# Retention, then SwiGLU on one core: operand stores a block earlier, a ring of four, wide float64 conversion

## The chip, the cores and the metric

One core of a Trainium2 chip runs the whole program. The metric is the device time of an execution in microseconds (us). Engines are named as in the profile: PE multiplies matrices, DVE, ACT and POOL work on elements, SP issues most of the DMAs.

## The reference

Two stages follow each other. For each of 4 batches and 8 heads the first carries a 64x64 state over 768 steps; the second is a SwiGLU block on 3072 rows of 512.

```python
for t in range(S):                       # q, k, v: (4, 8, 768, 64), float32
    state = gamma * state + outer(k[t], v[t])
    y[t] = scale * q[t] @ state          # gamma differs by head
x = y.transpose(0, 2, 1, 3).reshape(3072, 512)
g = x @ w_gate                           # 512 x 1536
out = (g / (1 + exp(-g)) * (x @ w_val)) @ w_out   # 1536 x 512
```

The three weights arrive as float64, everything else as float32.

## The kernel before

Retention runs on chunks of 128 steps. A segment is three chunks of two batches (six chunks, 768 rows of `xT`), and there are four segments. Each segment has a retention stage, an up stage of 12 blocks (one per 128 of the 1536 columns, `up`) and a down stage of three row groups (`down`). The retention of segment s+1 is cut into steps and put between the products of the down stage of segment s; that of segment 0 runs alone at the start.

The products are written as a Strassen-like scheme of seven: `up` multiplies seven operands (slots of a `wt` tile of 7 x 256) with seven activation operands (parts of `xT` and their sums `xs`, made in `sums_x`). In this text the products of a block are called by their order: first to seventh. First, third, fifth and seventh add into the PSUM tile `x`, second and fourth into `w`, sixth is `z`. Because `x` is added to again, the third product waits until ACT has copied the first result (`p1`), and the seventh until DVE has read `x` at line 381.

The float64 weights must become float32, and the slots that are sums must be formed. This happens in segment 0 only: a finished `wt` is stored to DRAM (`wstore`) and loaded again in segments 1 to 3 (`kept_wt`). A piece of 128x512 doubles is loaded as pairs of 32-bit words (`raw`), and `convert_piece` makes floats of it: one ACT operation on the low words (line 151), four on DVE (lines 153, 154, 158, 159) and an integer addition on POOL (line 161). `sums_t` then makes four sums on POOL (line 170). An up block has two such pieces (`w_gate`, `w_val`), and a half of a down operand `wot` (`w_out`) goes with it. `fill` puts these steps into the blocks of segment 0; each engine and each DMA queue works its instructions in the order of the program. `wt` tiles come from a ring of three, `raw` from a ring of two, and the store of block f's operands is issued after block f's products (line 487).

Of the kernel before, what the change touches and what calls it, by code (L numbers as in the profile page):

```python
# [37 lines left out]
def tile_retnet_swiglu(  # L38
# [45 lines left out]
    first = early.__enter__()  # L84
    ctx.enter_context(tc.manual_schedule())
# [36 lines left out]
    landed = {}  # L122

    def load_piece(n, dst, src):

        if src.dtype == F32:
            if len(src.shape) == 3:
                dst = dst.rearrange("p (c f) -> p c f", c=NC)
            nc.sync.dma_start(out=dst, in_=src)
            return  # L130
        raw = raws.tile([P, 2 * NC * P], U32, tag="raw", name=f"raw_{n}")
        to = raw.rearrange("p (c f) -> p c f", c=NC) if len(src.shape) == 3 else raw
        nc.sync.dma_start(out=to, in_=src.bitcast(U32))
        landed[n] = raw

    def convert_piece(n, dst):

        if n not in landed:
            return []
        raw = landed.pop(n).rearrange("p (n two) -> p n two", two=2)
        lo, hi = raw[:, :, 0], raw[:, :, 1]
        d = dst.bitcast(U32)

        def first_():  # L150
            nc.scalar.activation(lo.bitcast(F32), lo, AF.Copy, scale=2.0 ** -51,
                                 bias=2.0)
            nc.vector.tensor_scalar(d, hi, 0x7FFFFFFF, None, op0=ALU.bitwise_and)  # L153
            nc.vector.tensor_scalar(dst, dst, 122879.9921875, 2.0 ** -15,  # L154
                                    op0=ALU.min, op1=ALU.max)

        def second():
            nc.vector.tensor_scalar(hi, hi, 0x80000000, None, op0=ALU.bitwise_and)  # L158
            nc.vector.scalar_tensor_tensor(d, d, 3, hi, op0=ALU.logical_shift_left,  # L159
                                           op1=ALU.bitwise_xor)  # L160
            nc.gpsimd.tensor_tensor(dst.bitcast(I32), dst.bitcast(I32),  # L161
                                    lo.bitcast(I32), op=ALU.add)
        return [first_, second]

    def sums_t(w, b12):

        b11, b21, b22 = w[:, 0], w[:, 3 - b12], w[:, 3]
        t1, t3, t2, t4 = w[:, b12], w[:, 4], w[:, 5], w[:, 6]
        for o, a, b in ((t3, b22, t1), (t1, t1, b11), (t2, b22, t1), (t4, b21, t2)):
            nc.gpsimd.tensor_tensor(o, a, b, op=ALU.subtract)  # L170

    pieces = []

    def up_source(w, f):
        return w[:, ts(f, P)].rearrange("(c p) f -> p c f", p=P)

    for f in range(NF):
        pieces.append((f, 0, up_source(w_gate, f)))
        pieces.append((f, 1, up_source(w_val, f)))
    down_pieces = []  # L180
    for j in range(FH):
        for i in range(2):
            down_pieces.append((j, i, w_out[ts(j + FH * i, P)]))

    order = []
    for f in range(NF):
        order += [("up",) + pieces[2 * f], ("up",) + pieces[2 * f + 1]]
        order.append(("down",) + down_pieces[f])

    def place(n):  # L190
        kind, a, i, _ = order[n]
        if kind == "up":
            w = wt[0, a] if (0, a) in wt else new_wt(0, a)
        else:
            w = wot[a]
        return w, w[:, ds(2 * i, 2)].rearrange("p a b -> p (a b)")

    AHEAD = 2
    n_loaded = [0]

    def load_next():
        n = n_loaded[0]
        if n < len(order):
            n_loaded[0] += 1
            load_piece(n, place(n)[1], order[n][3])

    def steps_of_piece(n):

        kind, a, i, _ = order[n]

        def after():
            for s in todo[n]:
                s()
            load_next()
            if i == 1:
                sums_t(place(n)[0], 2 if kind == "up" else 1)

        todo = {}

        def one():  # L220
            steps = convert_piece(n, place(n)[1])
            todo[n] = steps[1:]
            for s in steps[:1]:
                s()
        return [one, after]

    fillers = [step for n in range(len(order)) for step in steps_of_piece(n)]

    def fill(k):
        for _ in range(min(k, len(fillers))):  # L230
            fillers.pop(0)()
# [48 lines left out]
    def state(c):  # L280
        ci = c % NCK
        if ci == NCK - 1:
            return
        kd = att.pop((c, "kd"))
        vn = chunks[c][3]
        st = bank("st", 1, f"st_{c}")
        for n in range(NP):
            nc.tensor.matmul(st[:, ts(n, P)], kd[:, ds(2 * n, 2)], vn[:, ts(n, P)],  # L288
                             start=(n == 0), stop=True, skip_group_check=True)
        new, old = state_of(c), state_of(c, 1)  # L290
        for i in range(2):
# [27 lines left out]
    def retention(s):  # L319
# [12 lines left out]
        for n, c in enumerate(cs):  # L332
# [3 lines left out]
            steps.append(lambda n=n: last(n))  # L336
        return steps
# [5 lines left out]
    def sums_x():  # L343
        s1, s2, s3, s4 = xs
        tt = nc.vector.tensor_tensor
        tt(s1, a_up(1, 0), a_up(1, 1), op=ALU.add)  # L346
        tt(s2, s1, a_up(0, 0), op=ALU.subtract)
        tt(s4, a_up(0, 1), s2, op=ALU.subtract)
        tt(s3, a_up(0, 0), a_up(1, 0), op=ALU.subtract)

    def up(s, f, fill):
# [10 lines left out]
        def tmp(nm):  # L362
            return io.tile([P, TH], F32, tag=nm, name=f"{nm}_{s}_{f}")
# [15 lines left out]
        tt(hT[:, f, 0], wb, u2, op=add)  # L379
        product(x, 4, s3, start=False)  # L380
        tt(hT[:, f, 1], x, p5, op=add)  # L381
        z = bank("wz", 2, f"z_{s}_{f}")[:, :TH]
        product(z, 1, a_up(0, 1))
        c11 = tmp("c11")
        tt(c11, z, p1, op=add)  # L385
        nc.scalar.activation(c11, c11, AF.Silu)  # L386
        fill(1)
        product(x, 6, a_up(1, 1), start=False)
        tt(hT[:, f, 0], hT[:, f, 0], c11, op=mul)  # L389
        sg = tmp("sg")  # L390
        nc.scalar.activation(sg, x, AF.Silu)
        fill(1)
        tt(hT[:, f, 1], hT[:, f, 1], sg, op=mul)
# [17 lines left out]
    def down(s, u, step):  # L411
# [10 lines left out]
        def tmp(nm):  # L422
            return io.tile([P, TH], F32, tag=nm, name=f"d{nm}_{s}_{u}")[:, :DH]
# [9 lines left out]
        product(x, 0, a_dn(0, 0, u))  # L433
        p1 = tmp("p1")
        nc.scalar.copy(p1, x)
        product(wb, 1, cur[1])
        p5 = tmp("p5")
        nc.scalar.copy(p5, wb)
        product(x, 5, cur[2], start=False)
        u2 = tmp("u2")  # L440
        nc.scalar.copy(u2, x)
        product(wb, 3, cur[4], start=False)
        tt(ev[0][:, DH:], wb, u2, op=ALU.add)
        more(1, 2, 4)
        product(x, 4, cur[3], start=False)
# [3 lines left out]
        product(z, 2, a_dn(0, 1, u))  # L449
        tt(ev[0][:, :DH], z, p1, op=ALU.add)  # L450
        product(x, 6, a_dn(1, 1, u), start=False)
# [10 lines left out]
    for n in range(1, len(cs)):  # L462
        load_chunk(cs[n], first, str(n))
        if n == 2:
            for _ in range(AHEAD):
                load_next()
    steps = retention(0)
    for n, st in enumerate(steps):
        st()
        if n >= 8 and n % 2 == 0 and len(fillers) > 2 * (len(order) - 6):  # L470
            fill(1)
    fill(len(fillers) - 2 * (len(order) - 6))
    sums_x()
# [3 lines left out]

    for s in range(NSEG):
        nxt = seg_chunks(s + 1) if s + 1 < NSEG else []
        for f in range(NF):  # L480
            if s:
                if f + 2 < NF:
                    kept_wt(s, f + 2)
            w = wt[s, f]
            up(s, f, fill if s == 0 else lambda k: None)
            if s == 0:
                nc.sync.dma_start(out=wstore[f], in_=w)
# [5 lines left out]

        def step():
            if steps:
                steps.pop(0)()

        for u in range(L):
# [3 lines left out]
            down(s, u, step)  # L502
        while steps:
            steps.pop(0)()
        if nxt:
            sums_x()
# [49 lines left out]
```

## Time and profile before

| what | us |
|---|---|
| median of 3 runs (877.7 to 881.0) | 880.84 |
| profiled execution, its own time | 879.36 |
| its span, first to last instruction | 877.6 |
| PE busy in the span | 780.5 |
| DVE, ACT, POOL busy | 372.9, 173.3, 158.1 |

The span is 1.76 us short of the execution's own time. Times in the rows are from the start of the span. The line numbers are those of the kernel before, except where the changed kernel is spoken of. A PEclk of 1.00 is 2.4 GHz and 0.50 is 1.2 GHz.

### The profile page before, as it was taken

The numbers are of one execution on the slowest core, as the hardware profiler recorded it, in microseconds if no ns is written. First come the engines' busy times: TensorE is split into PE (matmuls) and PEld (weight loads), VectorE is DVE, ScalarE is ACT, GpSimd is POOL, SyncE is SP. The second block draws the span as 40 slices with busy tenths as digits, with TensorE's granted clock in tenths as the row PEclk, the third lists the DMA queues.
The fourth block names the chain that finished last, engine by engine and source line by source line (L and its number), as shares of the span: only waits on it lengthen the run. The fifth ranks groups of instructions, "written<-read, shape, count | busy, mean of one in ns | idle before, by whom it ended". The sixth has DMA issues, their size and how long they took to land.

```text
span 877.6 us, 8898 instructions
## 1 busy us (share of the span) xinstructions
PE 780.5 (89%) x3440; PEld 542.7 (62%) x3440; DVE 372.9 (42%) x604; ACT 173.3 (20%) x350; POOL 158.1 (18%) x156
## 2 busy tenths in 40 slices
PE   6845766545699999999999999999999999999998
PEld 5623333223368887555578885555688875555787
DVE  3985644565545423333344532323454233323420
ACT  1222222212220011232210012222200112222100
POOL 2664544435431110000002200001011100000000
PEclk9867778777799999999999999999999999999999
DMA  9234434334442521232315302234025212321001
GB/s 342 78 100 137 135 117 155 135 115 137 171 164 84 204 80 66 85 114 96 137 37 205 127 25 84 86 124 173 8 84 204 78 66 84 107 103 43 1 25 48
DMA packets 38778, 95.74 MB, mean 109 GB/s; under 512 B 3280, under 2 KB 15568, under 8 KB 38736
## 3 DMA queue, kind: packets, MB, share of 16 engines
q1 hardware_dynamic: 35136, 88.09, 29.0%
q10 hardware_dynamic: 3600, 7.09, 2.3%
q8 instruction: 27, 0.44, 0.2%
q14 instruction: 15, 0.12, 0.0%
HBM read 77.86 MB, written 17.30 MB: 108 GB/s over the span
## 4 chain that ended last, share of the span: by engine, by line
PE 73%; DMA 1%; DVE 1%; issue 0%; SPq 0%; ACT 0%; DVEq 0%
PE x L359 23%; PE dx L418 15%; PE w L359 11%; PE dw L418 7%; PE z L359 6%; PE dz L418 4%; PE s L261 2%; PE y L314 2%; PE y L310 2%; PE st L288 1%; DMA wstore<-wt 1%; DVE wt L154 0%; DVE wt L153 0%; DVE wt L159 0%; DVE raw L158 0%
## 5 line engine op out<-in xcount | busy, mean ns | idle before, releaser
L359 PE MATMUL x<-xT,wt 128*128 128x384 f32 x384 | 155.6, 554 | 69.6 <-DVE hT L381 69.6
L359 PEld LDWEIGHTS x<-xT,wt 128*128 128x128 f32 x384 | 82.3, 218 | 132.4 <-issue 91.4
L359 PE MATMUL w<-xs,wt 128*128 128x384 f32 x384 | 141.6, 492 | 13.1 <-DVE xs L346 13.1
L359 PE MATMUL x<-xs,wt 128*128 128x384 f32 x384 | 140.9, 490 | 0.0
L359 PEld LDWEIGHTS w<-xs,wt 128*128 128x128 f32 x384 | 74.6, 195 | 67.2 <-POOL wt L170 14.5
L359 PEld LDWEIGHTS x<-xs,wt 128*128 128x128 f32 x384 | 73.5, 191 | 51.6 <-issue 1.2
L379 DVE TENSOR_TENSOR hT<-w,u 128x384 f32<-128x384 f32 x48 | 26.7, 557 | 153.8 <-PE w L359 153.8
L359 PE MATMUL z<-xT,wt 128*128 128x384 f32 x192 | 69.8, 486 | 0.0
L386 ACT ACTIVATE c<-c 128x384 f32<-128x384 f32 x48 | 25.1, 522 | 225.4 <-DVE c L385 225.4
L271 POOL TENSOR_TENSOR qd<-qt,tab 128x512 f32<-128x512 f32 x20 | 27.5, 1376 | 232.8 <-PE y L310 110.2
L418 PE MATMUL dw<-wot,hs 128*128 128x256 f32 x288 | 67.6, 384 | 0.0
L418 PE MATMUL dx<-wot,hs 128*128 128x256 f32 x288 | 67.0, 382 | 0.0
L418 PE MATMUL dx<-wot,hT 128*128 128x256 f32 x288 | 66.4, 381 | 0.0
L418 PEld LDWEIGHTS dx<-wot,hT 128*128 128x128 f32 x288 | 53.8, 190 | 8.5 <-issue 0.5
L418 PEld LDWEIGHTS dw<-wot,hs 128*128 128x128 f32 x288 | 53.2, 190 | 8.9 <-issue 1.5
L418 PEld LDWEIGHTS dx<-wot,hs 128*128 128x128 f32 x288 | 53.6, 190 | 8.0 <-issue 0.5
L275 POOL TENSOR_TENSOR kd<-kn,tab 128x512 f32<-128x512 f32 x20 | 20.9, 1044 | 195.2 <-DMA kn<-in_k_n_dram 110.4
L359 PEld LDWEIGHTS z<-xT,wt 128*128 128x128 f32 x192 | 36.5, 190 | 25.4
L161 POOL TENSOR_TENSOR wt<-wt,raw 128x512 int32<-128x512 int32 x24 | 31.2, 1298 | 86.7 <-DVE wt L159 60.2
L266 DVE TENSOR_TENSOR a<-s,tab 128x512 f32<-128x512 f32 x48 | 30.9, 685 | 32.3 <-PE s L261 32.2
L317 ACT COPY xT<-y 128x512 f32<-128x512 f32 x24 | 14.0, 585 | 149.6 <-PE y L314 149.6
L389 DVE TENSOR_TENSOR hT<-hT,c 128x384 f32<-128x384 f32 x48 | 32.0, 666 | 24.5 <-ACT c L386 24.5
(52 smaller groups left out, 765.8 us busy)
## 6 DMA issues: line engine op xcount, KB each, us to landing
wt<-wstore SPq DMA_DIRECT2D x36, 896.0 KB, 4.6
wstore<-wt SPq DMA_DIRECT2D x12, 896.0 KB, 5.9
kt<-in_k_t_dram SPq DMA_DIRECT2D x24, 256.0 KB, 5.0
qt<-in_q_t_dram SPq DMA_DIRECT2D x24, 256.0 KB, 5.2
kn<-in_k_n_dram SPq DMA_DIRECT2D x24, 256.0 KB, 5.4
vn<-in_v_n_dram SPq DMA_DIRECT2D x24, 256.0 KB, 4.5
raw<-in_w_gate_dram SPq DMA_DIRECT2D x12, 512.0 KB, 3.6
raw<-in_w_val_dram SPq DMA_DIRECT2D x12, 512.0 KB, 4.2
```

The source lines that it names most:

```text
L161: nc.gpsimd.tensor_tensor(dst.bitcast(I32), dst.bitcast(I32), lo.bitcast(I32), op=ALU.add)
L261: nc.tensor.matmul(sp[i][:, ts(n, P)], kt[r, n], qt[r, n], start=True, stop=True, skip_group_check=True)
L266: nc.vector.tensor_tensor(t, pairs(sp[i]), mask[:, i], op=ALU.mult)
L271: nc.gpsimd.tensor_tensor(qd, qt, qdec, op=ALU.mult)
L275: nc.gpsimd.tensor_tensor(kd, chunks[c][2].rearrange("p (h d) -> p h d", h=H), kdec[:, :, None].to_broadcast([P, H, D]), op=ALU.mult)
L310: nc.tensor.matmul(y[:, ts(n, P)], prev[:, n], qd[:, n], start=(n == 0), stop=False, skip_group_check=True)
L314: nc.tensor.matmul(y[ds(D * i, D), ts(n, P)], vn[:, ts(2 * n + i, D)], a[i][:, n], start=(ci == 0 and n == 0), stop=True, skip_group_check ...
L359: nc.tensor.matmul(o, w[:, slot, k], a[:, k], start=(start and k == 0), stop=(stop and k == KH - 1), skip_group_check=True)
L379: tt(hT[:, f, 0], wb, u2, op=add)
L386: nc.scalar.activation(c11, c11, AF.Silu)
L389: tt(hT[:, f, 0], hT[:, f, 0], c11, op=mul)
L418: nc.tensor.matmul(o, a[:, k], wot[k][:, slot], start=(start and k == 0), stop=(k == FH - 1), skip_group_check=True)
```

## The change

A piece is now a whole operand set of 128x1024 doubles: either an up block (`w_gate` and `w_val` together) or a whole `wot`. Its words land in one `raw` tile by three DMAs (up) or four (down), ordered so that the four converted slots lie side by side and two of the four sums are one instruction. Conversion has three stages: `convert_a` (two ACT operations), `convert_b` (two on DVE), `convert_c` (one on DVE, an addition on POOL, the sums, and for an up piece the store to `wstore`). The sums of a down piece move from POOL to DVE. Block f converts the operands of block f+2, in even blocks a `wot` too; ACT starts block f+1's pieces at the end of block f. The rings become four (`wt`) and three (`raw`). `sums_x` is done per row group inside the retention steps, the two last multiplications of a block (`hT` by `c11` and `sg`) are issued in the next block, the first state copy goes from DVE to ACT, and some buffers in `io` become single. `convert(f, 0)` stands behind the second product of a block, `convert(f, 1)` behind line 372.

```diff
+    def convert_a(piece):
+            nc.scalar.activation(d, hi.bitcast(F32), AF.Abs)
+            nc.scalar.activation(lo.bitcast(F32), lo, AF.Copy, scale=2.0 ** -51,
                                  bias=2.0)
...
+    def convert_b(piece):
+            nc.vector.tensor_scalar(d, d, 122879.9921875, 2.0 ** -15, op0=ALU.min,
+                                    op1=ALU.max)
             nc.vector.tensor_scalar(hi, hi, 0x80000000, None, op0=ALU.bitwise_and)
...
+    def convert_c(piece):
+            nc.vector.scalar_tensor_tensor(u, u, 3, hi, op0=ALU.logical_shift_left,
                                            op1=ALU.bitwise_xor)
+            nc.gpsimd.tensor_tensor(d.bitcast(I32), u.bitcast(I32), lo.bitcast(I32),
+                                    op=ALU.add)
...
+        sub = (nc.gpsimd if kind == "up" else nc.vector).tensor_tensor
...
+        sub(both, w[:, ds(B22, 2)], w[:, ds(B12, 2)], op=ALU.subtract)
+        sub(w[:, T2], w[:, B22], w[:, T1], op=ALU.subtract)
+        sub(w[:, T4], w[:, B21], w[:, T2], op=ALU.subtract)
         if kind == "up":
+            nc.sync.dma_start(out=wstore[a], in_=w)
...
+    at_block = [[("up", f + 2)] * (f + 2 < NF) + [("down", f // 2)] * (f % 2 == 0)
+                for f in range(NF)]
...
+    retain(8)
+    for p in order[:2]:
+        convert_a(p)
+        retain(2)
+        convert_b(p)
+        retain(2)
+        convert_c(p)
+        load_next()
+    for p in at_block[0]:
+        convert_a(p)
+    retain(len(steps))
...
+    def convert(f, part):
+        now = at_block[f]
+        if part == 0:
+            for p in now:
+                convert_b(p)
+            for p in now[:1]:
+                convert_c(p)
+                load_next()
+        else:
+            for p in now[1:]:
+                convert_c(p)
+                load_next()
+            if f + 1 < NF:
+                for p in at_block[f + 1]:
+                    convert_a(p)
...
-        tt(hT[:, f, 0], hT[:, f, 0], c11, op=mul)
-        sg = tmp("sg")
+        sg = tmp("sg", 1)
         nc.scalar.activation(sg, x, AF.Silu)
-        fill(1)
-        tt(hT[:, f, 1], hT[:, f, 1], sg, op=mul)
+        late.append(lambda: tt(hT[:, f, 0], hT[:, f, 0], c11, op=mul))
+        late.append(lambda: tt(hT[:, f, 1], hT[:, f, 1], sg, op=mul))
```

DVE, around block 2 of segment 0, before (`wt_4` is the operand tile of block 4, `wot_98` a down operand, `raw` the loaded words):

```order
L393 TENSOR_TENSOR hT<-hT,sg_1_585 128x384 [waits Activation_49]
L153 TENSOR_SCALAR wt_4_560<-raw_561 128x512 [waits DMAHW6_49,DMAHW0_49,PE_49]
L154 TENSOR_SCALAR wt_4_560<-wt_4_560 128x512 [waits DVE_49]
L158 TENSOR_SCALAR raw_561<-raw_561 128x512 [waits Pool_49]
L159 SCALAR_TENSOR_TENSOR wt_4_560<-wt_4_560,raw_561 128x512 [waits DVE_49]
L153 TENSOR_SCALAR wt_4_560<-raw_590 128x512 [waits DMAHW7_49]
L154 TENSOR_SCALAR wt_4_560<-wt_4_560 128x512 [waits DVE_49]
L158 TENSOR_SCALAR raw_590<-raw_590 128x512 [waits Pool_49]
L159 SCALAR_TENSOR_TENSOR wt_4_560<-wt_4_560,raw_590 128x512 [waits DVE_49]
L379 TENSOR_TENSOR hT<-w_2_599,u_0_2_618 128x384 [waits PE_49,Activation_49]
L381 TENSOR_TENSOR hT<-x_2_598,p_0_2_606 128x384 [waits PE_49]
```

The same block on DVE in the changed kernel (`wot_94` is the down operand of this block):

```order
L383 TENSOR_TENSOR hT<-hT,sg_1_561 128x384 [waits DVE_49,Activation_49]
L178 TENSOR_SCALAR wt_4_477<-wt_4_477 128x1024
L180 TENSOR_SCALAR raw_up_478<-raw_up_478 128x1024 [waits DMAHW6_49,DMAHW5_49,DMAHW4_49]
L178 TENSOR_SCALAR wot_94<-wot_94 128x1024
L180 TENSOR_SCALAR raw_down_497<-raw_down_497 128x1024 [waits DMAHW2_49,DMAHW7_49,DMAHW1_49,DMAHW0_49]
L188 SCALAR_TENSOR_TENSOR wt_4_477<-wt_4_477,raw_up_478 128x1024 [waits DVE_49]
L370 TENSOR_TENSOR hT<-w_2_564,u_0_2_592 128x384 [waits PE_49,Activation_49]
L372 TENSOR_TENSOR hT<-x_2_563,p_0_2_571 128x384 [waits PE_49]
L188 SCALAR_TENSOR_TENSOR wot_94<-wot_94,raw_down_497 128x1024 [waits DVE_49]
L198 TENSOR_TENSOR wot_94<-wot_94 128x2x256 [waits Pool_49]
L199 TENSOR_TENSOR wot_94<-wot_94 128x256 [waits DVE_49]
L377 TENSOR_TENSOR c_0_2_615<-z_2_612,p_0_2_567 128x384 [waits PE_49]
...
```

Before, the eight conversion steps stood ahead of lines 379 and 381, and the first of them waited for two DMAs. Now five wide ones stand ahead of lines 370 and 372, and the sums of the down operand, which wait for POOL, stand ahead of `c11` (line 377).

POOL in the same block, before and then in the changed kernel:

```order
L161 TENSOR_TENSOR wt_4_560<-wt_4_560,raw_561 128x512 [waits DMAHW0_49,DVE_49,DMAHW6_49,PE_49,Activation_49]
L161 TENSOR_TENSOR wt_4_560<-wt_4_560,raw_590 128x512 [waits DMAHW7_49,DVE_49,Activation_49]
L170 TENSOR_TENSOR wt_4_560<-wt_4_560 128x256 [waits Pool_49] x4
L161 TENSOR_TENSOR wot_98<-wot_98,raw_614 128x512 [waits DMAHW1_49,DVE_49,Activation_49]
L161 TENSOR_TENSOR wt_5_626<-wt_5_626,raw_627 128x512 [waits DMAHW2_49,DVE_49,DMAHW4_49,PE_49,Activation_49]
```

```order
L190 TENSOR_TENSOR wt_4_477<-wt_4_477,raw_up_478 128x1024 [waits DMAHW4_49,DMAHW5_49,DVE_49,DMAHW6_49,PE_49,Activation_49]
L198 TENSOR_TENSOR wt_4_477<-wt_4_477 128x2x256 [waits Pool_49]
L199 TENSOR_TENSOR wt_4_477<-wt_4_477 128x256 [waits Pool_49]
L200 TENSOR_TENSOR wt_4_477<-wt_4_477 128x256 [waits Pool_49]
L190 TENSOR_TENSOR wot_94<-wot_94,raw_down_497 128x1024 [waits DMAHW1_49,DMAHW2_49,DMAHW0_49,DMAHW7_49,DVE_49,Activation_49]
```

The addition of the down operand (the last row) stands behind the addition and the three sums of the up operand.

## Rows read from the trace of the kernel before

**Rows 1.** The page: busy tenths of PE and its clock in 40 slices.
```profile
PE   6845766545699999999999999999999999999998
...
PEclk9867778777799999999999999999999999999999
```
**Rows 2.** By stretch: length, busy PE, PEld, DVE, ACT, POOL, PEclk, DMA share, GB/s.
```profile
85.84:237.31 151.47, 91.89 (x224) 50.68 (x225) 82.67 (x137) 34.89 (x64) 70.32 (x73) 0.77 0.40 132
...
259.00:877.60 618.60, 614.71 (x2833) 441.88 (x2831) 224.03 (x366) 115.71 (x248) 34.15 (x28) 1.00 0.26 91
```
**Rows 3.** Waits in 60 to 240 us: total, times, longest.
```profile
PE x L359 <- DVE hT L381: 69.6, 10, 8.3
...
DVE wt L153 <- DMA wstore<-wt: 38.3, 5, 7.7
```
**Rows 4.** Timeline, blocks 3 and 8: start, length, engine, line, work [idle before <-releaser].
```profile
111.48 0.50 SPq L487 DMA_DIRECT2D wstore<-wt  x1
...
117.51 0.43 DVE L153 TENSOR_SCALAR wt<-raw 128x512 uint32<-128x512 uint32 x1 [7.63 <-DMA wstore<-wt]
117.97 0.43 DVE L154 TENSOR_SCALAR wt<-wt 128x512 f32<-128x512 f32 x1
...
123.39 5.46 PE L359 MATMUL x<-xT,wt 128*128 128x384 f32 x8 [7.61 <-DVE hT L381]
...
218.31 4.30 PE L359 MATMUL x<-xT,wt 128*128 128x384 f32 x8 [7.24 <-DVE hT L381]
```
**Rows 5.** Timeline of blocks 10 and 11, which convert nothing.
```profile
248.63 2.74 PE L359 MATMUL x<-xT,wt 128*128 128x384 f32 x8
...
250.64 0.56 DVE L393 TENSOR_TENSOR hT<-hT,sg 128x384 f32<-128x384 f32 x1
...
251.21 1.45 PE L359 MATMUL w<-xs,wt 128*128 128x384 f32 x4
```
**Rows 6.** Groups of instructions, shapes apart: busy us, mean ns.
```profile
L159 DVE SCALAR_TENSOR_TENSOR wt<-wt,raw 128x512 uint32<-128x512 uint32 x24 | 16.6, 693 | 0.8
...
L450 DVE TENSOR_TENSOR ev<-dz,dp 128x256 f32<-128x256 f32 x12 | 5.1, 423 | 10.1 <-PE dz L418 10.0
...
L151 ACT ACTIVATE raw<-raw 128x512 f32<-128x512 uint32 x36 | 24.3, 674 | 41.7 <-DMA raw<-in_w_val_dram 31.4 <-DMA raw<-in_w_gate_dram 4.0 <-DMA raw<-in_w_out_dram 3.6
...
L369 ACT COPY p<-x 128x384 f32<-128x384 f32 x48 | 22.9, 478 | 46.3 <-PE x L359 46.3
```
**Rows 7.** Timeline: POOL's addition and sums, alone and beside DVE.
```profile
103.46 1.28 POOL L161 TENSOR_TENSOR wt<-wt,raw 128x512 int32<-128x512 int32 x1 [1.48 <-issue]
...
104.82 3.58 POOL L170 TENSOR_TENSOR wt<-wt 128x256 f32<-128x256 f32 x4
...
106.74 1.07 DVE L389 TENSOR_TENSOR hT<-hT,c 128x384 f32<-128x384 f32 x1
...
130.09 3.14 POOL L170 TENSOR_TENSOR wot<-wot 128x256 f32<-128x256 f32 x4
```
**Rows 8.** One microsecond of PE's idle time: PE busy, PEclk, DMA share, GB/s.
```profile
118.00:119.00 1.00, 0.00 (x0) 0.95 0.00 0
```
**Rows 9.** Timeline of SP and PE at the start.
```profile
10.16 0.34 SPq L97 DMA_DIRECT2D kt<-in_k_t_dram  x1
...
10.84 0.34 SPq L97 DMA_DIRECT2D qt<-in_q_t_dram  x1
...
28.14 1.16 PE L261 MATMUL s<-qt,kt 64*128 64x128 f32 x16
...
37.78 2.05 PE L288 MATMUL st<-vn,kd 128*128 128x128 f32 x8 [2.30 <-POOL wt L170]
...
55.48 2.90 PE L359 MATMUL w<-xs,wt 128*128 128x384 f32 x4 [13.09 <-DVE xs L346]
```
**Rows 10.** Timeline of PE: second products of blocks 2 and 10.
```profile
91.09 1.71 PE L359 MATMUL w<-xs,wt 128*128 128x384 f32 x4
...
242.18 1.45 PE L359 MATMUL w<-xs,wt 128*128 128x384 f32 x4
```

More of the change, by code (lines that the diff above doesn't have):

```diff
@@ L136, in convert_piece, with load_piece @@
[L136 to L150, printed above, removed]
+    raw = {}
+    def load_piece(piece):
+        kind, a = piece
+        to = new_wt(0, a) if kind == "up" else wot[a]
+        if kind == "up":
+            halves = [w[:, ts(a, P)].rearrange("(c p) f -> p c f", p=P)
+                      for w in (w_gate, w_val)]
+            parts = [(halves[1][:, ds(KH, KH)], B22), (halves[1][:, ds(0, KH)], B12),
+                     (halves[0], B11)]
+        else:
+            top, low = (w_out[ts(a + FH * i, P)] for i in range(2))
+            parts = [(low[:, DH:], B22), (top[:, DH:], B12), (top[:, :DH], B11),
+                     (low[:, :DH], B21)]
+        if w_gate.dtype != F32:
+            raw[piece] = raws.tile([P, 4, 2 * KH * P], U32, tag="raw",
+                                   name=f"raw_{kind}{a}")
+        for src, slot in parts:
+            if w_gate.dtype == F32:
+                t = to[:, slot:]
+            else:
+                t, src = raw[piece][:, slot - B22:], src.bitcast(U32)
+            if len(src.shape) == 3:
+                c, f = src.shape[1:]
+                t = t.rearrange("p a b -> p (a b)")[:, : c * f]
+                t = t.rearrange("p (c f) -> p c f", c=c)
+            else:
+                t = t[:, 0]
+            nc.sync.dma_start(out=t, in_=src)
@@ L151, in first_, with words_of @@
+    def words_of(piece):
+        kind, a = piece
+        w = wt[0, a] if kind == "up" else wot[a]
+        d = w[:, ds(B22, 4)].rearrange("p a b -> p (a b)")
+        r = raw[piece].rearrange("p a (n two) -> p (a n) two", two=2)
+        return w, d, r[:, :, 0], r[:, :, 1]
+    def convert_a(piece):
+        if piece in raw:
+            w, d, lo, hi = words_of(piece)
+            nc.scalar.activation(d, hi.bitcast(F32), AF.Abs)
             nc.scalar.activation(lo.bitcast(F32), lo, AF.Copy, scale=2.0 ** -51,
@@ L163, in convert_piece @@
[L163 to L191, printed above, removed]
-        if kind == "up":
[L193 to L196, printed above, removed]
@@ L198, in tile_retnet_swiglu @@
-    AHEAD = 2
-    n_loaded = [0]
-    def load_next():
[L202 to L231, printed above, removed]
+    def convert_b(piece):
+        if piece in raw:
+            w, d, lo, hi = words_of(piece)
+            nc.vector.tensor_scalar(d, d, 122879.9921875, 2.0 ** -15, op0=ALU.min,
+                                    op1=ALU.max)
+            nc.vector.tensor_scalar(hi, hi, 0x80000000, None, op0=ALU.bitwise_and)
+    def convert_c(piece):
+        kind, a = piece
+        if piece in raw:
+            w, d, lo, hi = words_of(piece)
+            u = d.bitcast(U32)
+            nc.vector.scalar_tensor_tensor(u, u, 3, hi, op0=ALU.logical_shift_left,
+                                           op1=ALU.bitwise_xor)
+            nc.gpsimd.tensor_tensor(d.bitcast(I32), u.bitcast(I32), lo.bitcast(I32),
+                                    op=ALU.add)
+            del raw[piece]
+        w = wt[0, a] if kind == "up" else wot[a]
+        sub = (nc.gpsimd if kind == "up" else nc.vector).tensor_tensor
+        flat = w.rearrange("p a b -> p (a b)")
+        n = KH * P
+        both = flat[:, : 4 * n].rearrange("p (a b) -> p a b", b=2 * n)[:, :, :n]
+        sub(both, w[:, ds(B22, 2)], w[:, ds(B12, 2)], op=ALU.subtract)
+        sub(w[:, T2], w[:, B22], w[:, T1], op=ALU.subtract)
+        sub(w[:, T4], w[:, B21], w[:, T2], op=ALU.subtract)
+        if kind == "up":
+            nc.sync.dma_start(out=wstore[a], in_=w)
@@ L233, in tile_retnet_swiglu @@
+    at_block = [[("up", f + 2)] * (f + 2 < NF) + [("down", f // 2)] * (f % 2 == 0)
+                for f in range(NF)]
+    order = [("up", 0), ("up", 1)] + sum(at_block, [])
+    to_load = list(order)
+    def load_next():
+        if to_load:
+            load_piece(to_load.pop(0))
     mask = tab[:, MASK0:QDEC0].rearrange("p (i n t) -> p i n t", i=2, n=NP)
@@ L293, in state @@
             if ci == 0:
-                nc.vector.tensor_copy(out=new[r, :, r], in_=pairs(st)[r, :, r])
+                nc.scalar.copy(new[r, :, r], pairs(st)[r, :, r])
             else:
@@ L336, in retention @@
             steps.append(lambda n=n: last(n))
+            if n % 2:
+                steps.append(lambda n=n: sums_x(n // 2))
         return steps
@@ L341, in a_up, with sums_x, a, up @@
         return xT[:, ds(KH * j, KH), i]
-    def sums_x():
-        s1, s2, s3, s4 = xs
+    def sums_x(j):
+        def a(i, h):
+            return xT[:, ds(KH * h, KH), i, ts(j, P)]
+        s1, s2, s3, s4 = (t[:, :, ts(j, P)] for t in xs)
         tt = nc.vector.tensor_tensor
[L346 to L351, printed above, removed]
+        tt(s1, a(1, 0), a(1, 1), op=ALU.add)
+        tt(s2, s1, a(0, 0), op=ALU.subtract)
+        tt(s4, a(0, 1), s2, op=ALU.subtract)
+        tt(s3, a(0, 0), a(1, 0), op=ALU.subtract)
+    late = []
+    def up(s, f, convert):
         w = wt.pop((s, f)).rearrange("p o (k f) -> p o k f", k=KH)
@@ L420, in product, with tmp @@
             step()
-        def tmp(nm):
-            return io.tile([P, TH], F32, tag=nm, name=f"d{nm}_{s}_{u}")[:, :DH]
+        def tmp(nm, bufs):
+            return io.tile([P, TH], F32, tag=nm, name=f"d{nm}_{s}_{u}",
+                           bufs=bufs)[:, :DH]
         def more(*ns):
@@ L432, in down @@
         tt = nc.vector.tensor_tensor
[L433 to L434 removed]
+        product(x, B11, a_dn(0, 0, u))
+        p1 = tmp("p1", 2)
         nc.scalar.copy(p1, x)
[L436 to L437 removed]
+        product(wb, T1, cur[1])
+        p5 = tmp("p5", 1)
         nc.scalar.copy(p5, wb)
[L439 to L440 removed]
+        product(x, T2, cur[2], start=False)
+        u2 = tmp("u2", 1)
         nc.scalar.copy(u2, x)
[L442 removed]
+        product(wb, B22, cur[4], start=False)
         tt(ev[0][:, DH:], wb, u2, op=ALU.add)
         more(1, 2, 4)
[L445 removed]
+        product(x, T3, cur[3], start=False)
         tt(ev[1][:, DH:], x, p5, op=ALU.add)
@@ L448, in down @@
         z = bank("wz", 2, f"dz_{s}_{u}")[:, :DH]
-        product(z, 2, a_dn(0, 1, u))
+        product(z, B21, a_dn(0, 1, u))
         tt(ev[0][:, :DH], z, p1, op=ALU.add)
-        product(x, 6, a_dn(1, 1, u), start=False)
+        product(x, T4, a_dn(1, 1, u), start=False)
         nc.scalar.copy(ev[1][:, :DH], x)
@@ L463, in tile_retnet_swiglu, with retain @@
         load_chunk(cs[n], first, str(n))
-        if n == 2:
-            for _ in range(AHEAD):
-                load_next()
+        if n in (2, 3, 4):
+            load_next()
     steps = retention(0)
[L468 to L473, printed above, removed]
+    def retain(k):
+        for _ in range(k):
+            if steps:
+                steps.pop(0)()
+    retain(8)
[9 more added lines that the diff above has]
+    retain(len(steps))
     early.__exit__(None, None, None)
@@ L480, in tile_retnet_swiglu @@
         for f in range(NF):
[L481 to L487, printed above, removed]
+            if s and f + 2 < NF:
+                kept_wt(s, f + 2)
+            up(s, f, convert if s == 0 else lambda f, part: None)
+        while late:
+            late.pop(0)()
+        if s == 0:
+            raw_pool.__exit__(None, None, None)
+            loads = ctx.enter_context(
+                tc.tile_pool(name="loads", bufs=2, side="right"))
         for c in nxt[:2]:
@@ L501, in tile_retnet_swiglu @@
                 kept_wt(s + 1, 1)
[L502 to L506, printed above, removed]
+            down(s, u, lambda: retain(1))
+        retain(len(steps))
 def decay_table():
```

62 lines of the change are left out of this document (23 added, 39 removed).

## The prediction

> **What bounds the kernel now.** I read the page's slices first: PE is at nine tenths from the twelfth slice on, and before that at four to eight tenths with a clock of 0.6 to 0.9 [rows 1]. So the span falls in two. From 259 us to the end PE is busy for 614.7 of 618.6 us at full clock [rows 2], and only fewer matmuls could shorten that; the change leaves them as they are. The time to be had lies in segment 0, ahead of 259. There, from 85.84 to 237.31, eight blocks take 151.47 us, 18.93 each, with PE busy for 91.89 at a clock of 0.77 [rows 2]. The wait list names what ends PE's idle time: line 381 on DVE, ten times, 69.6 us [rows 3]. The timeline says why DVE is late: the store of a block's operands is issued at 111.48, DVE's first conversion step, which writes a ring slot still being stored, starts at 117.51, and lines 379 and 381 stand behind eight such steps, so that the seventh product starts at 123.39 after 7.61 us [rows 4]. Not every one of those waits is a DMA's by the list (38.3 us in 5), but the pattern repeats in each block. A block that converts nothing shows the floor: four records are one product, 1.29 us apart, seven products 9.03. The clock falls in the idle time (0.95 in the microsecond from 118 [rows 8]), and the two products behind the wait take 4.30 to 5.46 us [rows 4] against 2.74 [rows 5]: 1.6 to 2.7 lost, I take 2.2.
>
> **What goes.** The store leaves before the block that uses the operands, and the ring has a slot more, so the conversion finds its slot free: the 7.6 us wait has no ground left. Next in line are the conversion steps themselves. Two kinds of block alternate: odd ones convert an up piece, even ones an up piece and a whole down operand. PE needs ACT's first copy (p1) of a block before its third product, at 2.58, and line 372 before its seventh, at 7.74.
>
> **An even block, step by step**, from its first product at 0. DVE: the last multiplication of the block before ends at 1.28 (250.64 + 0.56, where the block began at 251.21 - 1.29 [rows 5]). Four 1024-wide tensor_scalars: 0.43 at 512 [rows 4], so between 0.43 (no growth) and 0.86 (twice); I take 0.70, nearer to twice, as only a fixed part doesn't grow: 2.8, to 4.1. Line 188: 0.69 at 512 and 0.42 at 256 [rows 6] make 0.27 per 256, so 1.22 at 1024 (bounds 0.69 and 1.39): 5.3. Lines 370 and 372 follow when PE delivers, at 7.2, in time for 7.74. POOL meanwhile: 0.2 to start; an addition over 1024 (1.28 at 512 [rows 7], bounds 1.28 and 2.56; by the step from 0.79 for one sum alone to 1.28, 2.3): 7.8; the three sums 1.3 + 0.8 + 0.8: 10.7; beside DVE the four sums took 3.58 instead of 3.14 [rows 7], so 0.5 more: 11.2. Only now comes the addition for the down operand, 2.3: 13.5. DVE has finished its own step for it at 8.5 and stands at line 198, which waits for POOL. **Behind it stands c11** (line 377), whose product has been ready since 7.8. DVE: 0.2 + 0.69 + 2 x 0.42 = 1.7, then c11 0.56: 15.8. On ACT the Silu of c11 waits for that, and behind it stand the Silu of sg and the next block's p1: 0.1 + 3 x 0.5 (0.48 for a copy [rows 6]): 17.4. So the next block's third product starts at 17.6 instead of 9.03 + 2.58 = 11.6: a new wait of 6.0 in each pair. Bounds, with every width at its ends: 13 and 19.5.
>
> The old waits of 7.2 to 7.6 took the clock down [rows 4]; for 6.0 I charge the same 2.2. A pair then takes 18.06 + 6.0 + 2.2 = 26.3, instead of 37.9. The odd block adds nothing: its POOL work begins at about 20.5 and ends near the pair's end, and its four ACT conversion steps (0.67 at 512 [rows 6], between that and 1.35; I take 1.1) fill ACT from 21 to 25.5, ahead of sg at 26.5.
>
> What a page of the Trainium skill says against the change: SBUF — State Buffer, "Who interferes with whom", holds that a DVE instruction with two SBUF inputs and a GpSimd instruction that reads SBUF lock each other out for a whole instruction. Line 188 of the down piece meets POOL's sums in just that way. By the page it would hold POOL up for up to its 1.22 us, so 0.7 more per pair than the 0.5 that I took, 3 us in four pairs. The trace agrees in kind, not in full size: line 389, two SBUF inputs, took 1.07 beside POOL's sums, which lost 0.44 [rows 7].
>
> **Traffic.** A pair moves two stores, two up pieces and a down piece, 4.8 MB; at 132 GB/s the share was 0.40 [rows 2], so 26.3 us at 183 GB/s are about 0.55. Three or four issues per piece at 0.34 [rows 9] cost SP nothing, as it waits most of the time.
>
> **The start.** Second products mark the blocks. Two more pieces are loaded before the last chunk: 2 MB at 0.67 per 256 KB (10.16 to 10.84 [rows 9]) are 5.4 us, most of it within slack; its scores move from 28.14 [rows 9] to 29. POOL's work for the first piece stands behind a chunk's kd, which waits for the product ahead of 28.14: 29.3; addition and sums 2.3 + 2.9 + 0.5: 35. Only then SP stores it, and loads the first down operand behind the store: 1.4 MB took 6.0 (111.48 to 117.51 with the piece issued just before), 0.5 MB more 1.3: 42.4. ACT has that operand's two steps (2.2) ahead of the last two copies to xT, and the last y waits for the first of those: 45.2. PE has idled, its clock is down: 24 matmuls at about 4 (8 took 2.05 [rows 9]), then 2.05 for the state: 51.3. DVE updates the state, 2.3, and makes the first sum, 0.42: the second product at 54.3, where it was 55.48 [rows 9]. So the early conversion gains 1.2 there (bounds: 8 gained if the operand lands at once, 5 lost).
> Block 0 then runs into the knot of an even block: sums to 55.6, conversion on DVE to 59.6, POOL 8.3 to 67.9, DVE and ACT 4.1 to 72.0 for block 1's third product; five products and the clock, 8.65: block 2 starts at 80.7, its second product at 82.0. It was 91.09 [rows 10]: 9.1 gained.
>
> **The sum.** Four pairs at 26.3 are 105.2, so block 10's second product comes at 187.2; it was 242.18 [rows 10]: 55.0 gained. Block 10 converts a down operand alone, with the whole chain ahead of line 372: 1.28 + 1.4 + 1.2 on DVE, 0.2 + 2.3 on POOL, 1.7 + 1.1 on DVE are 9.2, PE 0.2 later, and the seventh product was due at 7.74: 1.7 lost. Together 53.3.
> Everything later costs or gains nothing by my sum: sums_x, the deferred multiplications and the state copy move work between engines that idle half the time while PE is full [rows 2]; with three segment joins I bound that by 2 us either way. Span 877.6 - 53.3 = 824.3; with 1.76 around it 826.1, against 879.36 of the same execution and a median of 880.84. I say **826**. With the bounds of the pair (four times -4.6 to +1.9) and of the start it is 800 to 840.
>
> **Rivals.**
> - The new wait is short. If POOL's wide additions grow less than their width, the third product comes near 14.5, the clock holds, and a pair takes 21: 5.3 less four times, and about 5 in block 0: 800. For it: all these widths are extrapolated. Against it: five POOL instructions stand in a row ahead of c11 whatever their price.
> - Loads come late. The down operand is issued only when POOL has released a raw buffer, behind a store and an up piece, and ACT holds p1 behind it. If it lands 5 us later than reckoned, pairs take 31: 846. For it: the queue is in order and 1.4 MB took 6.0 us; against: eight microseconds pass before ACT asks.
> - Slower than before, by that same place: ACT at line 171 in every block, with loads, conversion and store of a piece in series. A pair would have to exceed 26.3 + 53.3/4 = 39.6, 13 us more, loads some 20 us from issue to landing: 890 at 42 a pair. No row has a landing half as long.
> - The change does not do what it says: a conversion still meets a store in flight, because the store itself waits for POOL's late sums. Then 7.6 us per block return, pairs near 36: 865.
>
> **How the numbers follow.** Forecast 0.70, short wait 0.15, late loads 0.10, store still met 0.02, slower 0.03. The range is 806 to 845: the forecast's bounds without the ends where every width is at its limit at once, half of the late loads, a little of the short wait. A difference of 0.5% (4.4 us) is what a measurement can tell here; only the slower case and a sliver lie beyond or near it, so faster 0.96, same 0.01, slower 0.03.
>
> **What would show it.** No wait on wstore at line 171 or 178; in even blocks DVE idle for 4 to 5 us before line 198 with POOL as releaser; PE's waits moved from the seventh product to the third of odd blocks, on ACT's p1; pairs of 25 to 28 us; the second product of block 0 within 50 to 58; the part after segment 0's up stage as long as before, 618 us. Wrong would be the whole if blocks run at 9.03 throughout, or if PE waits where ACT waits for raw.

## The result, and the profile after

The changed kernel takes 824.94 us (median of 4 runs, 823.77 to 826.29) against 880.68 for the kernel before: a ratio of 0.9375, 95% interval 0.9349 to 0.94. The profiled execution spans 822.6 us, 55.0 less than the 877.6 before.

The slices of the page (PE's busy tenths and its clock), as in [rows 1]: the full stretch begins in the tenth slice instead of the twelfth, and one slice ahead of it stands at a clock of 7 or less, where eight did.

```profile
PE   6566779779999999999999999999999999999997
...
PEclk9978899889999999999999999999999999999999
```

By stretch, as in [rows 2] (length, busy PE, PEld, DVE, ACT, POOL, clock, DMA share, GB/s): the four pairs of blocks, and all that follows the up stage of segment 0.

```profile
80.84:185.42 104.58, 82.81 (x226) 47.01 (x225) 57.17 (x90) 41.73 (x62) 53.85 (x36) 0.89 0.58 186
203.57:822.60 619.03, 614.76 (x2833) 442.00 (x2831) 226.12 (x386) 117.57 (x252) 33.48 (x28) 1.00 0.26 91
```

The second stretch is as long as it was (618.60), within 0.4. All of the gain lies ahead of it. The waits of 40 to 215 us (total, times, longest) stand against [rows 3]:

```profile
PE x L349 <- ACT p L359: 28.2, 5, 6.4
...
DVE wot L198 <- POOL wot L190: 28.1, 6, 5.1
...
ACT wt L171 <- DMA raw_up<-in_w_gate_dram: 13.2, 4, 4.6
...
PE y L292 <- POOL wt L199: 12.3, 1, 12.3
```

No row names wstore any more. PE's 69.6 us on DVE's line 381 have shrunk to 1.1 (now line 372, in block 10), and 28.2 us on ACT's p1 have come. The timeline of blocks 2 and 3 shows where (start, length, engine, line, work, idle before):

```profile
83.21 1.22 DVE L188 SCALAR_TENSOR_TENSOR wt<-wt,raw_up 128x1024 uint32<-128x1024 uint32 x1
...
84.65 2.39 POOL L190 TENSOR_TENSOR wt<-wt,raw_up 128x1024 int32<-128x1024 int32 x1 [5.29 <-DVE wt L188]
...
86.67 1.45 DVE L188 SCALAR_TENSOR_TENSOR wot<-wot,raw_down 128x1024 uint32<-128x1024 uint32 x1
...
87.12 2.13 POOL L198 TENSOR_TENSOR wt<-wt 128x512 f32<-128x512 f32 x1
...
90.83 2.37 POOL L190 TENSOR_TENSOR wot<-wot,raw_down 128x1024 int32<-128x1024 int32 x1
...
93.23 0.69 DVE L198 TENSOR_TENSOR wot<-wot 128x512 f32<-128x512 f32 x1 [5.11 <-POOL wot L190]
...
94.76 0.55 DVE L377 TENSOR_TENSOR c<-z,p 128x384 f32<-128x384 f32 x1
...
96.14 0.47 ACT L359 COPY p<-x 128x384 f32<-128x384 f32 x1
...
96.76 2.90 PE L349 MATMUL x<-xs,wt 128*128 128x384 f32 x4 [5.44 <-ACT p L359]
...
99.45 2.77 PE L349 MATMUL w<-xs,wt 128*128 128x384 f32 x4
...
102.01 1.54 PE L349 MATMUL x<-xs,wt 128*128 128x384 f32 x4
...
102.10 1.28 POOL L198 TENSOR_TENSOR wt<-wt 128x512 f32<-128x512 f32 x1
...
102.33 0.56 DVE L370 TENSOR_TENSOR hT<-w,u 128x384 f32<-128x384 f32 x1 [2.93 <-ACT raw_up L172]
...
107.26 1.45 PE L349 MATMUL w<-xs,wt 128*128 128x384 f32 x4
```

Read it downwards: POOL adds the up piece and makes its three sums, only then adds the down operand (90.83), DVE stands 5.11 us before line 198, `c11` (line 377) comes behind it, p1 behind that on ACT, and PE's third product last. The second products of blocks 0, 2 and 10, against [rows 9, 10]:

```profile
54.24 1.56 PE L349 MATMUL w<-xs,wt 128*128 128x384 f32 x4 [0.56 <-DVE xs L334]
...
80.84 1.45 PE L349 MATMUL w<-xs,wt 128*128 128x384 f32 x4
...
185.42 1.45 PE L349 MATMUL w<-xs,wt 128*128 128x384 f32 x4
```

### The profile page after: what moved, and what is told of

Same layout as the page of the kernel before. It is cut to its first block, busy times and chain, and to the rows that moved or that the text cites. A ratio compares the mean times of both kernels' runs of the same rounds, so it can differ in the third digit from the quotient of the medians.

```text
span 822.6 us, 8808 instructions
## 1 busy us (share of the span) xinstructions
PE 764.5 (93%) x3440; PEld 535.8 (65%) x3440; DVE 342.9 (42%) x556; ACT 190.7 (23%) x358; POOL 132.1 (16%) x102
## 4 chain that ended last, share of the span: by engine, by line
PE 77%; DVE 1%; POOL 0%; ACT 0%; issue 0%; DVEq 0%; ACTq 0%; POOLq 0%
PE x L349 24%; PE dx L408 15%; PE w L349 12%; PE dw L408 8%; PE z L349 6%; PE dz L408 4%; PE s L243 2%; PE y L296 2%; PE y L292 2%; PE st L270 2%; POOL wot L190 0%; DVE wot L198 0%; DVE wot L188 0%; ACT sg L381 0%; DVE wot L199 0%
## 5 line engine op out<-in xcount | busy, mean ns | idle before, releaser
L349 PE MATMUL x<-xs,wt 128*128 128x384 f32 x384 | 147.3, 508 | 28.2 <-ACT p L359 28.2
L349 PE MATMUL w<-xs,wt 128*128 128x384 f32 x384 | 144.0, 499 | 0.6 <-DVE xs L334 0.6
L349 PE MATMUL x<-xT,wt 128*128 128x384 f32 x384 | 132.4, 486 | 1.1 <-DVE hT L372 1.1
L349 PEld LDWEIGHTS x<-xs,wt 128*128 128x128 f32 x384 | 75.8, 199 | 83.4 <-issue 35.2
L349 PEld LDWEIGHTS x<-xT,wt 128*128 128x128 f32 x384 | 72.8, 190 | 51.4 <-issue 1.7
L370 DVE TENSOR_TENSOR hT<-w,u 128x384 f32<-128x384 f32 x48 | 26.8, 558 | 168.9 <-PE w L349 163.0
L280 DVE TENSOR_TENSOR state<-state,st 64x256 f32<-64x256 f32 x32 | 13.4, 418 | 67.2 <-PE st L270 66.3
L243 PE MATMUL s<-qt,kt 64*128 64x128 f32 x384 | 30.3, 298 | 11.7 <-DMA qt<-in_q_t_dram 8.3
```

Source lines behind the costliest of these rows:

```text
L243: nc.tensor.matmul(sp[i][:, ts(n, P)], kt[r, n], qt[r, n], start=True, stop=True, skip_group_check=True)
L349: nc.tensor.matmul(o, w[:, slot, k], a[:, k], start=(start and k == 0), stop=(stop and k == KH - 1), skip_group_check=True)
```

## The experiments

Each time is a median of four runs; behind it stand the ratio to the kernel before and its 95% interval. Every edit is made to the changed kernel. Lines behind an edit have moved: p1's copy is L357 to L372, line 372 is L370 to L385.

**Which part takes the old wait away: ring or early store?** Four kernels make a table: both, one, the other, none.

```diff
-    ring = ctx.enter_context(tc.tile_pool(name="ring", bufs=4))
+    ring = ctx.enter_context(tc.tile_pool(name="ring", bufs=3))
```

> A ring of three with the early store. Theory: ACT's first conversion step for block f+3 writes the slot of block f and must wait for that block's last product; in odd blocks four ACT steps then stand ahead of p1, 3 to 5 us more PE wait per pair: about 845. Rival (the early store alone suffices): 822 to 828.

842.59 us, 0.9581 (0.9556 to 0.9606). The waits have no row on wstore. ACT now stands at line 171 for PE's last reading of the slot, with p1 behind it:

```profile
ACT wt L171 <- PE x L349: 49.6, 9, 5.9
PE x L349 <- ACT p L359: 39.1, 9, 6.4
```

The other part undone, ring of four:

```diff
-        if kind == "up":
-            nc.sync.dma_start(out=wstore[a], in_=w)
...
+            w = wt[s, f]
+            if s == 0:
+                nc.sync.dma_start(out=wstore[f], in_=w)
```

> The store of block f's operands goes back behind block f's products in the program, the ring stays four. Theory: with a slot more the store has landed a few us before ACT writes its slot again, so no new wait, and the loads, no longer behind a store, help the start by some 4: 818 to 828. Rival (the early issue of the store is what took the old wait away): ACT waits for wstore at line 171, 2 to 6 us per block, 845 to 870.

822.1 us, 0.9344 (0.9316 to 0.9373). ACT now meets the store for 1.6 us a block (12.9 in 8), PE's waits for p1 are 5.6 to 6.8, and block 0's second product comes at 49.56 instead of 54.24, as the down operand's load no longer stands behind a store. So two effects nearly cancel: against the changed kernel 4.7 us are gained ahead of block 2 (its second product at 76.13 instead of 80.84) and 4.0 lost in the four pairs (108.58 instead of 104.58). Both edits together:

> Ring of three and the store behind the block's products, both as in the kernel before, with the rest of the change kept. Theory: the wait for wstore is back, now on ACT at line 171, some 9 us per pair: 855 to 875. Rival (the wide conversion alone brings the gain): 822 to 835.

897.46 us, 1.021 (1.0183 to 1.0238): some 2% slower than the kernel before, and outside what either theory gave.

```profile
ACT wt L171 <- DMA wstore<-wt: 107.0, 7, 18.9
...
PE x L347 <- ACT p L357: 84.0, 7, 16.5
```

So the ring of four is what matters, 75 us with a late store and 17.7 with an early one. With it the early store changes the time by nothing that the intervals can tell from zero; with a ring of three it brings 55. And what else the change does is, without either, slower than the old order: the first conversion step that writes the slot is now ACT's, so the wait for the store stands in front of p1. The kernel before with nothing but a ring of four was not run, so how much of the gain the wider conversion brings stays open.

**Is the new wait made by line 198 ahead of c11?** Three ways to free `c11`. The down sums behind `c11` of the next block:

```diff
+        if kind == "up":
+            sums(piece)
+        else:
+            owed.append(piece)
...
+        if s == 0 and f % 2:
+            while owed:
+                sums(owed.pop(0))
```

> The three DVE sums of a down operand move behind c11 of the next (odd) block. Theory (c11 stands behind sums that wait for POOL): PE's wait for p1 in odd blocks goes, 5.4 us and the half clock behind it; what comes next is the landing of the next pieces (load, two ACT steps, two DVE steps, POOL, store, load again: about 21 us per pair), so a pair falls from 26.2 to about 21.5 and the time to about 800. Rival (ACT's waits for raw words hold p1, the sums only fill that time): pairs stay near 26, time 820 to 827.

812.36 us, 0.9231 (0.9212 to 0.9251). The wait is gone from the third product of odd blocks, and 18.6 us of the same name have come in even ones. A pair takes 23.9 to 27.1 us instead of the expected 21.5. The timeline shows why:

```profile
122.06 1.16 ACT L171 ACTIVATE wt<-raw_up 128x1024 f32<-128x1024 f32 x1 [6.00 <-DMA raw_up<-in_w_gate_dram]
...
124.74 1.12 ACT L171 ACTIVATE wot<-raw_down 128x1024 f32<-128x1024 f32 x1 [0.49 <-DMA raw_down<-in_w_out_dram]
...
127.53 0.48 ACT L368 COPY p<-x 128x384 f32<-128x384 f32 x1
...
128.15 2.55 PE L358 MATMUL x<-xs,wt 128*128 128x384 f32 x4 [4.37 <-ACT p L368]
```

ACT waits for the raw words, and p1 stands behind four conversion steps. The same sums behind `c11` of their own block:

```diff
+        while s == 0 and owed:
+            sums(owed.pop(0))
```

> The same three sums directly behind c11 of their own block. Theory: c11 is free, but DVE now stands at the sums until POOL's last addition, so the conversion of the odd block is late and with it lines 370 and 372: PE waits some 3 us for line 372 in odd blocks instead of 5.4 for p1; pair 23 to 24, time 808 to 815. Rival (only c11 counts): as good as moving the sums a block later, about 800. Rival (ACT's loads): 820 to 827.

812.69 us, 0.9224 (0.9202 to 0.9247): line 372 of the odd block is late instead (13.3 us in 4). The sums back on POOL:

```diff
-        sub = (nc.gpsimd if kind == "up" else nc.vector).tensor_tensor
+        sub = nc.gpsimd.tensor_tensor
```

> The sums of the down operand go back from DVE to POOL, as in the kernel before. Theory: DVE has nothing to wait for ahead of c11, so the wait for p1 in odd blocks goes; POOL ends the pair's work 3 us later, so stores and loads are later and PE waits for ACT behind late words for part of it: pair about 22, time about 803. Rival (POOL is the true bound): pair 27 or more, time 826 or more.

812.62 us, 0.9227 (0.9205 to 0.9248), PE waiting 14.1 us for line 372 and ACT 36.9 for raw words. All three gain 12 to 13 us and lose the wait of 5.4 us at the third product of odd blocks (0.4 to 2.2 remain there in the second and third): line 198's place did set it. But their pairs still take 24.8 to 25.3 on the mean (26.15 before the edit; the rest of the gain lies ahead of block 2 and behind block 10): a second limit lies close under the first. That is why the first and the third of these kernels miss the 800 and 803 that their theories gave.

**Is that second limit the loads behind the store?** The next piece's loads are issued ahead of the store:

```diff
-            nc.sync.dma_start(out=wstore[a], in_=w)
+            stores.append(a)
...
+        while stores:
+            a = stores.pop(0)
+            nc.sync.dma_start(out=wstore[a], in_=wt[0, a])
```

> Only the queue is changed: the next piece's loads are issued ahead of the store of the operands. Theory (c11 knot sets the pair): ACT waits less for raw words, PE as long as before: 820 to 826. Rival (late loads hold p1): 3 us per pair, 805 to 812.

819.55 us, 0.9312 (0.9293 to 0.933). The pairs keep their 5.43 to 5.45 us of wait; all the gain is ahead of block 2 (block 0's second product at 49.64). With the sums moved as in the first of the three:

> The down sums a block later (as in e1) and the loads ahead of the store (as in e8) together. Theory (two limits behind one another: first c11, then the landing of the words that ACT waits for ahead of p1): alone they gave 12.6 and 5.4; together more than the sum, since only now the landing sets the pair: pairs near 22, about 795. Rival (the two gains just add): 807. Rival (DVE or POOL is full): no better than e1, 812.

797.72 us, 0.9058 (0.9039 to 0.9077). Alone the edits gain 12.6 and 5.4, together 27.2: two limits, one under the other. Pairs take 22.4 to 22.6 us. The timeline shows what is left of the waits. Behind the one that ends at 95.14 the products run at full speed (1.53 and 1.46); behind the one that ends at 117.63 they do not (1.86 and 2.77, with a granted clock of 0.50, that is 1.2 GHz, from 119 to 122):

```profile
88.89 2.82 PE L362 MATMUL x<-xT,wt 128*128 128x384 f32 x8 [1.61 <-DVE hT L385]
...
95.14 1.53 PE L362 MATMUL x<-xs,wt 128*128 128x384 f32 x4 [2.13 <-ACT p L372]
...
96.50 1.46 PE L362 MATMUL w<-xs,wt 128*128 128x384 f32 x4
...
117.63 1.86 PE L362 MATMUL x<-xs,wt 128*128 128x384 f32 x4 [2.08 <-ACT p L372]
...
119.28 2.77 PE L362 MATMUL w<-xs,wt 128*128 128x384 f32 x4
```

**The start.** ACT takes block 0's down operand behind the last copies to xT:

```diff
-    for p in at_block[0]:
-        convert_a(p)
+    convert_a(at_block[0][0])
     retain(len(steps))
+    convert_a(at_block[0][1])
```

> At the start ACT converts the first down operand behind the last copies to xT instead of ahead of them. Theory: the last y waited for ACT's copy of the y before, which stood behind the landing of that operand; now it starts when POOL's qd is there, near 39 instead of 47.5 us, the second product of block 0 comes at about 48 instead of 54.2, and the whole gains 5 to 7: about 818. Rival (POOL's sums, which the trace names as the releaser, hold y): no change, 823 to 826.

819.72 us, 0.9321 (0.9299 to 0.9343); block 0's second product at 49.84 instead of 54.24. In the changed kernel the profile puts PE's wait down to POOL's line 199, which ended at 47.46, but ACT's copy of the y before ended at 47.39 (first three rows; the fourth is of the kernel with the edit):

```profile
46.68 0.78 POOL L199 TENSOR_TENSOR wt<-wt 128x256 f32<-128x256 f32 x1
46.82 0.57 ACT L299 COPY xT<-y 128x512 f32<-128x512 f32 x1
...
47.53 2.05 PE L292 MATMUL y<-qd,state 128*128 128x128 f32 x8 [12.26 <-POOL wt L199]
```

```profile
37.79 1.16 PE L292 MATMUL y<-qd,state 128*128 128x128 f32 x8 [3.12 <-POOL qd L253]
```

The edit leaves POOL's order alone, and PE starts 9.7 us sooner, 8.3 ahead of POOL's line 199 (46.06), so ACT's copy held it.

**Can the pair reach its floor?** The up sums also wait until POOL has added the down operand, so that their stores are late too; with the start's edit:

```diff
+        owed.append(piece)
...
+        if s == 0 and f % 2:
+            sums("down")
...
                 convert_c(p)
                 load_next()
+            sums("up")
```

> As e5, with POOL adding the down operand ahead of the up operand's sums (so its raw buffer is free and its load out 3 us sooner), and the first down operand converted behind the copies to xT (as in e7). Theory: no wait of PE beyond a us per block in segment 0, pairs 18.1 to 20, the second product of block 0 near 49: 778 to 790. Rival (landing still sets the pair): 795 to 800. Rival (DVE, some 15 us busy of 18 and locked out beside POOL, sets it): waits for line 372, about 800.

796.91 us, 0.9045 (0.9023 to 0.9068), the fastest of all, and 3.4% below the changed kernel, yet not apart from the 797.72 by the intervals. The floor of 18.06 isn't reached; pairs take 22.2 to 22.5, and PE waits for line 372 nine times, 13.1 us in all (from 60 to 200 us), as the last rival had it. In its timeline line 188 of the down operand, 1.22 alone, takes 2.83 beside POOL's addition:

```profile
98.14 1.21 DVE L188 SCALAR_TENSOR_TENSOR wt<-wt,raw_up 128x1024 uint32<-128x1024 uint32 x1
...
99.58 2.38 POOL L190 TENSOR_TENSOR wt<-wt,raw_up 128x1024 int32<-128x1024 int32 x1 [4.65 <-DMA wstore<-wt]
...
100.21 2.83 DVE L188 SCALAR_TENSOR_TENSOR wot<-wot,raw_down 128x1024 uint32<-128x1024 uint32 x1
100.43 2.82 PE L360 MATMUL x<-xT,wt 128*128 128x384 f32 x8 [1.20 <-DVE hT L383]
...
104.10 1.88 DVE L395 TENSOR_TENSOR hT<-hT,c 128x384 f32<-128x384 f32 x1 [0.59 <-ACT c L391]
```

DVE's step ends at 103.04, 1.08 behind the end of POOL's (101.96). (POOL's row names a store as releaser, but POOL starts 0.23 behind the end of line 188 of the up piece, at 99.35, as in the changed kernel: 84.43 to 84.65.) By its records DVE is full, 87.23 of 90 us against 50.78 in the changed kernel. By the lengths of the pairs (22.25 and 26.15 on the mean) that is 21.6 and 14.8 us a pair for the same instructions, so part of it is standing:

```profile
72.00:162.00 90.00, 76.09 (x228) 42.20 (x227) 87.23 (x90) 42.27 (x63) 55.96 (x37) 1.00 0.60 204
```

A last kernel moves the two line 188 steps, the up piece's behind line 372 and the down operand's behind `c11`, with POOL's work behind them. One theory had their order as the limit, the other the exclusion between DVE and POOL:

```diff
         c11 = tmp("c11", 2)
         tt(c11, z, p1, op=add)
+        convert(f, 2)
```

> As e15, but DVE does the up piece's wide step (line 188) behind lines 370 and 372 and the down piece's behind c11. Theory 1 (only the order on DVE made line 372 late in e15): the waits of 1 to 2 us for line 372 go, pairs 18.5 to 20, 778 to 788. Theory 2 (POOL and DVE's instructions with two SBUF inputs shut each other out: 13 us of POOL and up to 11.6 us of such DVE work in a pair): the wait only moves, pairs stay 21 to 22.5, 792 to 800.

802.79 us, 0.9117 (0.9102 to 0.9132): 5.9 slower than the kernel without this move, and a little outside both theories' ranges. The waits for line 372 stay (13.8 us in nine), and pairs take 20.8 to 24.8 us, so it was not this order alone that made line 372 late.

```profile
104.36 2.39 POOL L190 TENSOR_TENSOR wt<-wt,raw_up 128x1024 int32<-128x1024 int32 x1 [5.58 <-DMA wstore<-wt]
104.53 3.31 DVE L188 SCALAR_TENSOR_TENSOR wot<-wot,raw_down 128x1024 uint32<-128x1024 uint32 x1
```

Again DVE ends 1.09 behind POOL (107.84, 106.75), and POOL starts 0.22 behind the up piece's line 188 (104.14), whatever its row names. That fits the exclusion but does not show it to be the limit: a kernel without any overlap of the two was not run, so how much of the 4 us that a pair takes above its floor comes from it stays open.

## Why the prediction was right

- **What goes.** As said: no wait on wstore in the changed kernel. The step spoke of store and ring together; the table parts them. An early store with a ring of three also ends the wait on wstore, but the slot is then still being read by PE (49.6 us on ACT in nine waits); a late store with a ring of four leaves 12.9 us in eight. The slot more is what the time needs.
- **The even block.** From its first product (1.29 before 80.84, 79.55) the steps fell where they were put: POOL's first addition ends at 7.49 (7.8 predicted), its sums at 11.32 (11.2), the down addition at 13.65 (13.5), `c11` at 15.76 (15.8), the third product at 17.2 (17.6). It was due at 11.6, so 5.6 are lost where 6.0 were reckoned (the record of the wait has 5.44, as the product before it is recorded 0.16 longer than the step to the next).
- **The widths.** 0.69 for the tensor_scalar (0.70), 1.22 for line 188 (1.22), 2.39 to 2.42 for POOL's addition (2.3), as these groups of the changed kernel have them (busy, mean ns):

```profile
L190 POOL TENSOR_TENSOR wt<-wt,raw_up 128x1024 int32<-128x1024 int32 x12 | 29.0, 2417 | 67.8 <-issue 34.9 <-DVE wt L188 32.9
...
L188 DVE SCALAR_TENSOR_TENSOR wt<-wt,raw_up 128x1024 uint32<-128x1024 uint32 x12 | 14.7, 1222 | 0.2
...
L178 DVE TENSOR_SCALAR wot<-wot 128x1024 f32<-128x1024 f32 x6 | 4.1, 686 | 0.0
```

- **DVE beside POOL** was charged 0.5 and cost POOL's first sum 0.85 (2.13 at 87.12 against 1.28 alone at 102.10). DVE's line 188 had itself waited: it ended at 88.12, 1.08 behind POOL's addition (87.04), and POOL's sum ended 1.13 behind that. The Trainium skill, SBUF — State Buffer, "Who interferes with whom", has the later of the two blocked fully; here the trace agrees nearly in size too: POOL's sum stood for 1.00 (87.12 to 88.12), under the bound of 1.22, and then took 1.13 where it takes 1.28 alone.
- **The clock.** The two products behind the wait begin 5.25 apart (96.76 to 102.01) instead of 2.58, with a granted clock of 0.50 (1.2 GHz) from 96.76 to 102.00: 2.67 lost, 2.2 charged. It differs by pair: from the third product to the next block's second, 7.74 at full clock, the four took 10.50 (96.76 to 107.26), 9.24, 10.30 and 10.84, so 2.5 are lost on the mean. The pair then comes to 18.06 + 5.6 + 2.5 = 26.2; the four took 104.6, 26.15 each, against 26.3. A wait 0.4 too long and a clock 0.3 too cheap nearly cancel.
- **The start** came out at 54.24 for 54.3, but by luck, as two errors cancel. ACT had the operand at 44.77, not 42.4: POOL's addition began at 31.04 instead of 29.3 and stood longer beside DVE. Behind it only 6.7 us were needed to the second product (47.53 to 54.24), not the 9.1 reckoned from 45.2: the state's product took 1.16 rather than 2.05, and from its end to the second product 1.85 passed instead of 3.0, as DVE had a step of its update done.

```profile
29.85 1.22 POOL L257 TENSOR_TENSOR kd<-kn,tab 128x512 f32<-128x512 f32 x1
...
31.04 2.58 POOL L190 TENSOR_TENSOR wt<-wt,raw_up 128x1024 int32<-128x1024 int32 x1
...
31.84 2.33 DVE L178 TENSOR_SCALAR wt<-wt 128x1024 f32<-128x1024 f32 x1
...
44.77 1.13 ACT L171 ACTIVATE wot<-raw_down 128x1024 f32<-128x1024 f32 x1 [13.04 <-DMA raw_down<-in_w_out_dram]
...
51.23 1.16 PE L270 MATMUL st<-vn,kd 128*128 128x128 f32 x8
```

- **The sum.** Gained up to block 2: 10.25 (9.1); the four pairs: 46.5 (45.9); block 10 and 11 lost 1.4 (1.7); the rest lost 0.4 (nothing). Together 55.0, predicted 53.3.
- **Traffic.** A share of 0.58 at 186 GB/s in the four pairs, against about 0.55 at 183.
- **The rivals.** "The new wait is short" fell with the widths, and "a conversion still meets a store" with the waits, which have no row on wstore. "Late loads" didn't decide here, since ACT asked late enough, but they are what came next: with `c11` free ACT waits at line 171 (e1's timeline). "Slower, ACT at line 171 in every block" is near to what a ring of three with the late store does, 897 us against the 890 reckoned, though there ACT waits for the store and not for loads.

## What to carry to other kernels

When a wait on an in-order engine is taken away, ask of each engine what else stands in its queue ahead of what the critical engine needs; here it was a DVE step that waits for POOL, then ACT steps that wait for loads. Two limits may lie close under each other, so try cures together as well as alone: 12.6 and 5.4 made 27.2. And when a conversion moves to another engine, its wait for a buffer moves too, and may stand in front of something dearer.

## What was not expected of the hardware

Line 188 on DVE, a scalar_tensor_tensor over 1024 with both inputs in SBUF (1.22 alone), started beside POOL's addition in the three places shown: it took 1.45, 2.83 and 3.31 us and ended 1.08 to 1.09 behind POOL's end each time. A tensor_scalar of 0.69 did the like at the start (2.33 at 31.84, ending 0.55 behind POOL's 33.62). Each time what was left to do behind the other engine's end was 0.13 to 0.15 less than the instruction takes alone (1.08 of 1.22, 1.13 of 1.28, 0.55 of 0.69). Line 370, one of whose inputs is in PSUM, took its usual 0.56 beside POOL's sum (102.33, inside 102.10 to 103.38). The time that an engine stands in this way is recorded as busy, so that a DVE that looks full may be one that waits.
